# Attention pieces in another order: the value product one unit behind the transposes, the next scores behind it, weight conversions placed one by one

## The chip, the core and the metric

The kernel runs on one core of a Trainium2 chip. The engines named below are PE (TensorE, matrix products), DVE (VectorE), ACT (ScalarE), POOL (GpSimd) and SP (which issues most transfers). Each engine works through its own list of instructions in the order in which the list is written, and waits on semaphores for the others. The metric is the device time of one execution in microseconds (us), lower is better.

## The reference

Three stages: attention with a window of 32 tokens and 32 global tokens per batch, a dense layer with a gated activation, and a routed layer of eight experts.

```python
# attention, B=4, H=8, 512 local and 32 global tokens, head size 64
s_g = scale * q_g @ k_all^T;  out_g = softmax(s_g) @ v_all      # global rows see every key
s_l = concat(scale * q_l @ k_g^T, where(|i-j| <= 32, scale * q_l @ k_l^T, -1e9))
out_l = softmax(s_l) @ concat(v_g, v_l)
x = concat(out_g, out_l)                    # 2304 tokens x 512
# dense layer, 512 -> 2048 -> 512
h = x @ w_in
sp = where(h > 20, h, log1p(exp(min(h, 20))))
y = (h * tanh(sp)) @ w_out
# routed layer: each token goes to one expert, 288 tokens to each
logits = y @ w_gate                         # assigned greedily over the sorted logits
out[mask_e] = relu(y[mask_e] @ w1[e]) @ w2[e]
```

## The kernel before

**Phase 1** does the attention and, between its parts, the first half of the dense layer's 2048 columns. The attention is cut into 24 **pieces**: 16 local ones (128 queries each, `piece`) and 8 global ones (one batch and four heads, `piece_g`). A piece is a Python generator that stops at lettered stages: `q` scores on PE (tile psS), `t` mask and row minimum on DVE (P, mx), `e`/`f` eight exponentials on ACT, `n` row sums inverted on DVE (sm), `a`/`A` transposes of heads 0 to 3 on PE (psA) and their copy on ACT (PAA), `b`/`B` the same for heads 4 to 7 (PAB), `v` value product on PE (psO), `x` scaling on DVE (O), `z` transposes of O on PE (psX) and the split into a high part (ACT, x0h) and a low part (DVE, x0l). In a global piece the tiles are Pg, PgA, PgB and Og. psA has one buffer, so the second transposes wait for the first copy; psO and psX share one buffer.

The dense layer is cut into **chunks**: 256 tokens times 256 hidden columns. A chunk is four **units** of PE work: two of the first product (`m1a`, tiles psH<-x..,wi..; 12 matmuls each) and two of the second (`m1b`, psY<-wo..; 6 matmuls each). Between them stands a chain over ACT and DVE: exponential (me), two DVE steps (mu), Ln and exponential on ACT, two DVE steps (mu, mw), the split into gh (ACT) and gl (DVE). The second product of a chunk comes after the first product of the next one. `gate` steps (psrT, psl) work out routing logits of finished rows.

The dense weights come as 64-bit words and are turned into floats by `load_wide`: a transfer into a staging buffer (wide, three buffers), three DVE steps (wz, L228 to L230), then a high part on ACT (L203) and a low part on POOL (L206). Phase 1 needs 16 such loads: two each of w_in and w_out for four pairs of columns (wi00, wo00 to wi03, wo03).

**What sets the order.** In phase 1 every PE instruction is linked behind the one before it, as the code emits it. For the first three pieces ACT and DVE are linked in the same way; after that a scheduler places their instructions by what they depend on. The order of emission is a string: SEQ0 for each of the first three pieces, SEQ for the rest. `0` is the new piece, `1` the one before it; `w` are two dummy matmuls, `u` one unit, `U` units as long as some are due (5.2 for a local, 3.0 for a global piece), `g` a gate step, and `s` starts one more weight load and advances all that are under way by a step. SP issues transfers in order and waits in that order: `load_qk(t + 2)` stands behind the scores of piece t and waits for them, `load_v(t + 2)` behind the value product of piece t.

**After phase 1** come phase 2 (the rest of the dense layer), the routing and the experts.

Of the kernel before, what the change touches and what calls it, by code (L numbers as in the profile page):

```python
# [15 lines left out]
OP = mybir.AluOpType  # L16
# [3 lines left out]
B, H, SL, SG, D = 4, 8, 512, 32, 64  # L20
# [20 lines left out]
PE, ACT, DVE = mybir.EngineType.PE, mybir.EngineType.Activation, mybir.EngineType.DVE  # L41
LINK = [PE]
WARM = 10
GLOBALS = (4, 5, 8, 10, 11, 12, 13, 14)
CH0 = 3
RATE = {"l": 5.2, "g": 3.0}
LAG = 1
XTRA = 3
WK = 2
CHAIN = 5  # L50
SEQ0 = "0q w 1A 0t w 1B 1v s 0e w 1x 0f 1z s 0n"
SEQ = "u 1A 0n u s 1B 1v u s g u 1x g u s 1z g U"
STAGES = "qtefnaAbBvxyz"
NS = 3
SIDE = "oo ooo - o oo - - i ii i ii - ii"
LOAD_AT = 1
STEP_FILL = 8
# [93 lines left out]
class Build:  # L151
# [158 lines left out]
    def step(s, *new, mid=None):  # L310
# [10 lines left out]
        s.gate((0,))  # L321
        s.turn_all(s.side)

    def link(s, x):
        if s.order is not None and x.ins.engine in s.linked:
            if x.ins.engine in s.order:
                s.tc.add_manual_dep(x.ins, s.order[x.ins.engine],
                                    mybir.DependencyInfo(mybir.DependencyClass.NoSync, mybir.DependencyReason.DATA),
                                    reason="pipeline")
            s.order[x.ins.engine] = x.ins.name  # L330
        return x

# [22 lines left out]
    def piece(s, t):  # L355
        nc = s.nc
        c = t % 4
        qk = s.Q[t]
        mask = s.mask[:, 0 if c == 0 else (2 if c == 3 else 1)]
        pool = s.psE[t % len(s.psE)]  # L360
        psS = [pool.tile([128, 4, 128], F32, name="psS") for _ in range(2)]
        for hp in range(4):
            for u, f in enumerate(FIRST):
                r = slice(u * 32, u * 32 + 32)
                for j in range(2):
                    q = qk[j * 64:(j + 1) * 64, hp]
                    s.link(nc.tensor.matmul(psS[j][r, hp], q[:, r], q[:, 128 + f * 32:256 + f * 32], start=True, stop=True))  # L367
        s.load_qk(t + 2)
        yield "q"
        P = s.ap.tile([128, 8, 128], F32, name="P", bufs=2)  # L370
        mx = s.sp.tile([128, 8], F32, name="mx")
        sm = s.sp.tile([128, 8], F32, name="sm")
        for h in range(8):
            s.link(nc.vector.tensor_tensor_reduce(out=P[:, h], in0=psS[h % 2][:, h // 2], in1=mask, scale=-SCALE, scalar=3e38,  # L374
                                                  op0=OP.add, op1=OP.min, accum_out=mx[:, h:h + 1]))
        yield "t"
        for h in range(8):
            s.link(nc.scalar.activation(P[:, h], P[:, h], AF.Exp, bias=mx[:, h:h + 1], scale=-1.0,  # L378
                                        accum_out=sm[:, h:h + 1]))
            if h == 3:  # L380
                yield "e"
        yield "f"
        s.link(nc.vector.tensor_scalar(sm, sm, 1e-9, None, op0=OP.add))
        s.link(nc.vector.reciprocal(sm, sm))
        yield "n"
        PT = []
        for z, (y, w) in enumerate(("aA", "bB")):
            ps = s.psT.tile([128, 4, 128], F32, name="psA", tag="t")
            for h in range(4):
                s.link(nc.tensor.transpose(ps[:, h], P[:, 4 * z + h], s.ident))  # L390
            yield y
            PT.append(s.ap.tile([128, 4, 128], F32, name="PA" + "AB"[z], tag="P" + "AB"[z], bufs=1))
            s.link(nc.scalar.activation(PT[z], ps, AF.Copy))  # L393
            yield w
        psO = s.psT.tile([128, 8, D], F32, name="psO", tag="x")
        v = s.V[t]
        for h in range(8):
            for u in range(4):
                r = slice(u * 32, u * 32 + 32)
                s.link(nc.tensor.matmul(psO[r, h], PT[h // 4][:, h % 4, r], v[:, u, h * D:(h + 1) * D], start=True, stop=True))  # L400
        s.load_v(t + 2)
        yield "v"
        O = s.ap.tile([128, 8, D], F32, name="O", bufs=1)
        s.link(nc.vector.tensor_tensor(O, psO, sm[:, :, None].to_broadcast([128, 8, D]), op=OP.mult))  # L404
        yield "x"
        px = s.psT.tile([128, 4, 128], F32, name="psX", tag="x")
        for hp in range(4):
            s.link(nc.tensor.transpose(px[:, hp], O[:, 2 * hp:2 * hp + 2].rearrange("p h d -> p (h d)"), s.ident))  # L408
        bi, col = min(t // 2, 7), t - 2 * min(t // 2, 7)
        if bi < 7 and col == 0:  # L410
            s.X[bi] = s.xslots(bi % 3)
        cs = slice(col * 128, col * 128 + 128)
# [31 lines left out]
    def piece_g(s, i):  # L444
# [143 lines left out]
    def phase1(s, p1):  # L588
        nc, tc = s.nc, s.tc
        s.Q, s.V, s.X, s.x_d, s.ready, s.ys = {}, {}, {}, {}, set(), {}  # L590
        pieces = []
        for t in range(16):
            pieces += [("l", t)] + [("g", i) for i, a in enumerate(GLOBALS) if a == t]
        chunks = [(bi, f) for bi in range(6) for f in range(0, FP, 2)]
        with ExitStack() as at:
# [20 lines left out]
            nc.sync.dma_start(s.ident, s.ins["cst"][:, :128])  # L616
            s.load_qk(1)
            s.load_v(0)
            loads = [z for i in range(4) for ld in (s.load_in, s.load_out) for z in ld(0, i, lambda i=i: s.w1[i])]
            s.X[7] = s.xslots(7, 384)  # L620
            s.order, s.linked = {}, [PE, ACT, DVE]
# [25 lines left out]

            n = 0
            acc = 0.0
            old = []  # L650
            while pieces or old:
                s.turn_all(s.tails)
                if n == XTRA:
                    extra.close()
                    s.psE = [s.psS]
                    s.psY = [p1.enter_context(tc.tile_pool(name="psY", bufs=2, space=PSUM, side="right"))] * 2
                p = pieces.pop(0) if pieces else ("g", None)
                new = None if p[1] is None else s.piece(p[1]) if p[0] == "l" else s.piece_g(p[1])
                acc = min(acc + RATE[p[0]], 8) if n >= CH0 else 0
                old[:0] = [new]  # L660
                if n == NS:
                    s.linked, s.static = LINK, False
                cur = 0
                for op in (SEQ0 if n < NS else SEQ).split():
                    if op == "w":
                        idle(WK)
                    elif op == "s":
                        if loads:
                            s.side.append(loads.pop(0))
                        s.turn_all(s.side)  # L670
                    elif op == "u":
                        if acc >= 1 and unit():
                            acc -= 1
                    elif op == "U":
                        while acc >= 1 and unit():
                            acc -= 1
                    elif op == "g":
                        cur = s.gates[0] if s.gates and cur == 0 else cur
                        k = s.at.get(cur, 0)
                        if cur in s.gates:  # L680
                            s.gate((k,))
                            if k == 0:
                                s.gate((1,))
                        cur = cur or None
                    elif int(op[0]) < len(old) and old[int(op[0])]:
                        g = old[int(op[0])]
                        while STAGES.index(op[1]) > at_stage.get(g, -1):
                            at_stage[g] = STAGES.index(next(g, "z"))
                del old[1:]
                if new is None:  # L690
                    old = []
                if n == 0:
                    s.load_v(1)
                    nc.sync.dma_start(s.wg[:, :4 * E].rearrange("p (k e) -> p k e", e=E), s.ins["wg"].rearrange("(k p) e -> p k e", p=128))
                if n == 3:
                    s.load_gk(0)
                    s.load_gv(0)
                n += 1
            assert not loads
            for c, what, _ in units:  # L700
                r = next(c, 0)
                if what is None:
# [536 lines left out]
```

## Time and profile before

| | |
|---|---|
| median of three runs | 871.46 us (868.78 to 872.36) |
| the profiled execution | 868.8 us, span 867.0 us |
| PE busy | 777.0 us, 90% of the span |
| DVE, ACT, POOL busy | 537.8, 429.5, 168.6 us |
| mean granted clock of PE | 0.950 of full speed |
| end of phase 1 (first matmul on x7 after the last piece) | 316.78 us |

The span runs from the first to the last instruction. A row of the chronological view gives the start, the duration, the engine, the line, the operation and its tiles, and in brackets the idle time before it and what ended that. A row of the view of waits gives the total, how often, and the longest. Granted clock 1.00 is 2.4 GHz, and 0.5 would be 1.2 GHz.

### The profile page before, as it was taken

To read this page: it belongs to the slowest core of one execution; us is meant where nothing else is said; L and a number is where in the kernel's file an instruction comes from. 1 tells how busy PE (TensorE), PEld (TensorE's weight loads), DVE (VectorE), ACT (ScalarE), POOL (GpSimd) and SP (SyncE) were. 2 spreads that over 40 slices of the span, in tenths; PEclk is the share of its full clock that TensorE was granted. 3 is DMA by queue.
4 is the path that set the end of the run, shared out by engine and by line. 5 is a ranking of instruction groups with operands and counts; after the bars stand their busy time and mean duration, and the time that the engine had idled before them with its cause. 6 is when DMAs were issued, how large, how long until landed. Compare 5 with 4: busy or idle time off the path is not lost. (4 is left out here: it accounts for less than half of the span.)

```text
span 867.0 us, 18491 instructions
## 1 busy us (share of the span) xinstructions
PE 777.0 (90%) x7496; PEld 675.3 (78%) x7496; DVE 537.8 (62%) x1323; ACT 429.5 (50%) x955; POOL 168.6 (19%) x138
## 2 busy tenths in 40 slices
PE   5767897889998999989999997899879899999995
PEld 2555776767777778878999976677679899999995
DVE  2687755535555548887878767887646555555420
ACT  3465466536565647455656553212246454554420
POOL 0222100000000012143100137634340211222001
PEclk9787899979999999999999999899999999999998
DMA  9879564626543102243113115332467657666101
GB/s 347 316 275 318 182 220 169 238 71 215 198 173 118 42 26 73 74 146 110 50 50 98 50 40 150 50 37 37 110 196 221 197 172 246 196 215 198 50 1 60
DMA packets 44726, 124.30 MB, mean 143 GB/s; under 512 B 5728, under 2 KB 14432, under 8 KB 42592
## 3 DMA queue, kind: packets, MB, share of 16 engines
q1 hardware_dynamic: 37696, 103.45, 35.6%
q0 software_dynamic: 6944, 19.67, 8.9%
q8 instruction: 59, 0.97, 0.5%
q14 instruction: 27, 0.22, 0.1%
HBM read 103.43 MB, written 19.66 MB: 142 GB/s over the span
## 5 line engine op out<-in xcount | busy, mean ns | idle before, releaser
L519 ACT ACTIVATE me<-psH 128x512 f32<-128x512 f32 (+1 forms) x72 | 41.1, 571 | 82.0 <-PE psH L511 79.1
L521 DVE TENSOR_SCALAR mu<-me 128x512 f32<-128x512 f32 (+1 forms) x72 | 34.5, 479 | 55.7 <-ACT me L519 54.6
L378 ACT ACTIVATE P<-P,mx 128x128 f32<-128x128 f32 x128 | 49.5, 388 | 12.8 <-DVE mx L374 12.8
L527 DVE TENSOR_TENSOR mu<-mu,psH 128x512 f32<-128x512 f32 (+1 forms) x72 | 47.0, 653 | 12.3 <-ACT me L524 11.6
L524 ACT ACTIVATE me<-mu,two 128x512 f32<-128x512 f32 (+1 forms) x72 | 49.9, 694 | 8.1 <-DVE mu L522 7.6
L522 DVE SCALAR_TENSOR_TENSOR mu<-me,mu 128x512 f32<-128x512 f32 (+1 forms) x72 | 47.6, 662 | 2.2
L1193 DVE SCALAR_TENSOR_TENSOR hl<-ps2H,hh 128x272 fp32r<-128x272 f32 x64 | 27.2, 437 | 28.6 <-ACT hh L1192 28.4
L1192 ACT ACTIVATE hh<-ps2H 128x272 fp32r<-128x272 f32 x64 | 24.7, 394 | 40.3 <-PE ps2H L1190 40.3
L206 POOL TENSOR_TENSOR wo10l<-wz,wo10h 128x512 fp32r<-128x512 f32 x2 | 2.5, 1289 | 216.7 <-ACT wo10h L203 216.7
L525 ACT ACTIVATE me<-me 128x512 f32<-128x512 f32 (+1 forms) x72 | 43.7, 607 | 1.6
L374 DVE CUSTOM_DVE_ANT_0 P<-psS,mask 128x128 f32<-128x128 f32 x128 | 28.7, 284 | 13.8 <-PE psS L367 13.7
L1171 POOL DMA_INDIRECT out<-ro,idx x17 | 21.9, 1289 | 60.0 <-ACT ro L1170 46.3
L1207 ACT ACTIVATE oT<-ps2O 128x256 f32<-128x256 f32 x32 | 12.1, 378 | 43.1 <-PE ps2O L1205 43.1
L537 DVE TENSOR_TENSOR gl<-mw,gh 128x512 fp32r<-128x512 f32 (+1 forms) x36 | 27.0, 751 | 6.7 <-ACT gh L535 6.1
L1208 DVE COPY orest<-ps2O 128x16 f32<-128x16 f32 x32 | 5.5, 172 | 38.9 <-ACT oT L1207 38.9
L529 DVE TENSOR_TENSOR g<-mu,me 128x512 f32<-128x512 f32 (+1 forms) x36 | 27.2, 755 | 3.9 <-ACT me L525 0.3
L535 ACT ACTIVATE gh<-mw 128x512 fp32r<-128x512 f32 (+1 forms) x36 | 21.7, 603 | 11.6 <-DVE mw L534 11.2
L408 PE MATMUL psX<-ident,O 128*128 128x128 f32 x64 | 11.9, 317 | 16.7 <-DVE O L404 16.7
L400 PE MATMUL psO<-v,PAB 128*32 128x64 f32 x512 | 11.3, 233 | 17.1 <-ACT PAB L393 16.6
L534 DVE TENSOR_TENSOR mw<-mu,me 128x512 f32<-128x512 f32 (+1 forms) x36 | 25.0, 693 | 2.1 <-ACT me L525 0.8
L228 DVE TENSOR_SCALAR wz<-wide 128x512 int32<-128x512 int32 x32 | 16.7, 522 | 14.4 <-DMA wide<-w_in 10.3
L229 DVE SCALAR_TENSOR_TENSOR wz<-wide,wz 128x512 int32<-128x512 int32 x32 | 24.8, 774 | 0.3
(933 smaller groups left out, 2964.3 us busy)
## 6 DMA issues: line engine op xcount, KB each, us to landing
stage<-w SPq DMA_DIRECT2D x64, 512.0 KB, 4.0
v<-v SPq DMA_DIRECT2D x16, 1024.0 KB, 5.3
qk<-qk SPq DMA_DIRECT2D x16, 960.0 KB, 5.4
wide<-w_in SPq DMA_DIRECT2D x16, 512.0 KB, 3.7
wide<-w_out SPq DMA_DIRECT2D x16, 512.0 KB, 4.0
kgl<-kt SPq DMA_DIRECT2D x8, 544.0 KB, 4.1
vgl<-vt SPq DMA_DIRECT2D x8, 512.0 KB, 5.7
y_d<-y1o SPq DMA_DIRECT2D x16, 256.0 KB, 2.8
```

Source lines behind the costliest of these rows:

```text
L374: s.link(nc.vector.tensor_tensor_reduce(out=P[:, h], in0=psS[h % 2][:, h // 2], in1=mask, scale=-SCALE, scalar=3e38, op0=OP.add, op1=OP.mi ...
L378: s.link(nc.scalar.activation(P[:, h], P[:, h], AF.Exp, bias=mx[:, h:h + 1], scale=-1.0, accum_out=sm[:, h:h + 1]))
L519: s.link(nc.scalar.activation(e, ps, AF.Exp))
L521: s.link(nc.vector.tensor_scalar(u, e, E20, 2.0, op0=OP.min, op1=OP.add))
L522: s.link(nc.vector.scalar_tensor_tensor(u, e, E20, u, op0=OP.min, op1=OP.mult))
L524: s.link(nc.scalar.activation(e, u, AF.Ln, bias=s.two))
L525: s.link(nc.scalar.activation(e, e, AF.Exp, scale=-1.0))
L527: s.link(nc.vector.tensor_tensor(u, u, ps, op=OP.mult))
L529: s.link(nc.vector.tensor_tensor(w, u, e, op=OP.mult))
L534: s.link(nc.vector.tensor_tensor(w, u, e, op=OP.mult))
L537: s.link(nc.vector.tensor_tensor(gl, w, gh.bitcast(F32), op=OP.subtract))
L1193: nc.vector.scalar_tensor_tensor(hl[:, f], ps, 0.0, hh[:, f].bitcast(F32), op0=OP.max, op1=OP.subtract)
```

## The change

The parts of the pieces are emitted in another order. In the steady order (SEQ) a unit now stands between the first transposes and the second (`1A g u 1B`), another between the second transposes and the value product (`1B g c c u g 1v`), the scores of the next piece come behind the value product (`1v 1x 0q`) and no longer between the two transposes, and two units stand between these scores and the transposes of O. The addition and reciprocal of the row sums move from stage `n` to behind the value product. Each of the first three pieces has a string of its own. The loads of weights are started, converted and split by three letters of their own (`i`, `c`, `k`), two at a time, instead of by `s`. The global pieces come earlier (behind local pieces 3, 4, 6, 8, ... instead of 4, 5, 8, 10, ...), and two loads (the second v, the first global piece's) are issued earlier.

```diff
-GLOBALS = (4, 5, 8, 10, 11, 12, 13, 14)
+GLOBALS = (3, 4, 6, 8, 10, 11, 12, 13)
...
-SEQ0 = "0q w 1A 0t w 1B 1v s 0e w 1x 0f 1z s 0n"
-SEQ = "u 1A 0n u s 1B 1v u s g u 1x g u s 1z g U"
+SEQ0 = ["i i 0q w 0t w 0f w", "0q w 0t 1A w 1B w 1v 0f 1x c k 1z c k i i",
+        "1A w 1B w 1v 1x 0q 0t c k 1z 0f c k i i u u"]
+SEQ = "1A g u 1B g c c u g 1v 1x 0q k k 0n i i u u c c 1z k k i i U"
...
+    def behind(s, x, name):
+        s.tc.add_manual_dep(x.ins, name if isinstance(name, str) else name.ins.name,
+                            mybir.DependencyInfo(mybir.DependencyClass.NoSync, mybir.DependencyReason.DATA),
+                            reason="pipeline")
...
         yield "f"
-        s.link(nc.vector.tensor_scalar(sm, sm, 1e-9, None, op0=OP.add))
-        s.link(nc.vector.reciprocal(sm, sm))
         yield "n"
...
+                last = s.link(nc.tensor.matmul(psO[r, h], PT[h // 4][:, h % 4, r], v[:, u, h * D:(h + 1) * D], start=True, stop=True))
         s.load_v(t + 2)
         yield "v"
+        s.behind(s.link(nc.vector.tensor_scalar(sm, sm, 1e-9, None, op0=OP.add)), last)
+        s.link(nc.vector.reciprocal(sm, sm))
...
-                    elif op == "s":
+                    elif op == "i":
                         if loads:
-                            s.side.append(loads.pop(0))
-                        s.turn_all(s.side)
+                            wide.append((loads.pop(0), 0))
+                            next(wide[-1][0])
+                    elif op in "ck":
+                        for k, (g, at) in enumerate(wide):
+                            if at == "ck".index(op):
+                                wide[k] = g, at + 1
+                                next(g, 0)
+                                break
```

**PE, a local piece between two local pieces.** First before, in the middle of phase 1; psS are the scores of the next piece, psA the two transposes of the current one, PAA and PAB the two halves of its value product, psX its last transposes:

```order
L390 MATMUL psA<-ident,P 128x128 x4
L367 MATMUL psS<-qk 32x128 x32
L545 MATMUL psY<-wo03h,gh 128x512
...
L390 MATMUL psA<-ident,P 128x128 x4
L400 MATMUL psO<-v,PAA 32x64 x16
L400 MATMUL psO<-v,PAB 32x64 x16
L545 MATMUL psY<-wo03h,gh 128x512
...
L511 MATMUL psH<-x2h,wi01l 128x256
L408 MATMUL psX<-ident,O 128x128 x4
```

The same stretch of the program now, for another local piece (line numbers of the changed kernel):

```order
L391 MATMUL psA<-ident,P 128x128 x4
L284 MATMUL psl<-rT,wg 32x128 x4
L514 MATMUL psH<-x1h,wi02h 128x256
...
L288 MATMUL psl<-ident,gT 128x128
L401 MATMUL psO<-v,PAA 32x64 x16
L401 MATMUL psO<-v,PAB 32x64 x16
L370 MATMUL psS<-qk 32x128 x32
L514 MATMUL psH<-x1h,wi02h 128x256
...
L548 MATMUL psY<-wo01h,gl 128x512
L411 MATMUL psX<-ident,O 128x128 x4
```

A unit has moved in between the second transposes and the value product, the scores have moved behind the value product, and two units follow them before psX.

**ACT, the copies PAA and PAB.** Before, at a local piece in the middle of phase 1 (P,sm are exponentials of the next piece, me, gh are the dense chain):

```order
L393 ACTIVATE PAA<-psA 128x512
L524 ACTIVATE me<-mu,two 128x512
L525 ACTIVATE me<-me 128x512
L378 ACTIVATE P,sm<-P,mx 128x128
L535 ACTIVATE gh<-mw 128x512
L378 ACTIVATE P,sm<-P,mx 128x128 x7
L393 ACTIVATE PAB<-psA 128x512
```

Now, at a local piece (rT, gT belong to the gate steps):

```order
L394 ACTIVATE PAA<-psA 128x512
L527 ACTIVATE me<-mu,two 128x512
L279 ACTIVATE rT<-psrT 128x512
L528 ACTIVATE me<-me 128x512
L394 ACTIVATE PAB<-psA 128x512
L286 ACTIVATE gT<-psl 128x128
L538 ACTIVATE gh<-mw 128x512
L381 ACTIVATE P,sm<-P,mx 128x128 x8
```

The eight exponentials of the next piece stood ahead of PAB and now stand behind it.

**SP, the loads around the third pair of w_in.** Now (v and qk are loads of local pieces, kgl and vgl of a global one, wide are weight loads, x_d stores of finished rows); the first row shown is the load of the fifth v:

```order
L350 DMA v<-v 128x2048
L345 DMA qk<-qk 128x1920
L223 DMA wide<-w_out 128x1024 x2
L223 DMA wide<-w_in 128x4x256
L350 DMA v<-v 128x2048
L223 DMA wide<-w_in 128x4x256
L431 DMA qg<-qg 128x64
L433 DMA kgl<-kt 128x1088
L223 DMA wide<-w_out 128x1024 x2
L223 DMA wide<-w_in 128x4x256
L420 DMA x_d<-x1h 128x1024
L223 DMA wide<-w_in 128x4x256
```

The second half of wi02 has the load of the sixth v ahead of it (before it was the fifth), and the second half of wi03 has a store of x1 ahead of it.

## Rows read from the trace of the kernel before

**Rows 1.** Busy time, granted clock, DMA share, GB/s of each engine in five stretches.
```profile
0.00:40.00 40.00, 24.17 (x392) 14.76 (x393) 17.43 (x76) 16.41 (x59) 5.28 (x8) 0.83 0.91 336
40.00:97.00 57.00, 41.93 (x599) 35.06 (x599) 44.20 (x119) 31.85 (x90) 14.62 (x11) 0.79 0.80 281
97.00:200.00 103.00, 88.34 (x1200) 72.84 (x1199) 53.76 (x173) 55.94 (x160) 1.29 (x1) 0.92 0.48 168
200.00:316.00 116.00, 108.59 (x1564) 87.15 (x1562) 66.79 (x206) 72.13 (x202) 0.00 (x0) 0.99 0.39 135
316.00:336.00 20.00, 19.02 (x120) 16.68 (x123) 11.34 (x25) 12.62 (x27) 3.54 (x3) 1.00 0.14 44
```

**Rows 2.** What PE waited for from 5 to 316 us: total, times, longest.
```profile
PE psX L408 <- DVE O L404: 16.7, 4, 8.5
PE psO L400 <- ACT PAB L393: 16.6, 9, 3.9
PE psO L488 <- ACT PgB L480: 7.5, 7, 1.5
```

**Rows 3.** ACT in order of time, 140 to 152 us.
```profile
143.87 0.40 ACT L378 ACTIVATE P<-P,mx 128x128 f32<-128x128 f32 x1 [0.30 <-DVE mx L374]
...
147.31 0.39 ACT L378 ACTIVATE P<-P,mx 128x128 f32<-128x128 f32 x1
...
147.70 0.57 ACT L393 ACTIVATE PAB<-psA 128x512 f32<-128x512 f32 x1
```

**Rows 4.** PE in order of time, three rows from three places of phase 1.
```profile
23.65 1.11 PE L408 MATMUL psX<-ident,O 128*128 128x128 f32 x4 [8.49 <-DVE O L404]
...
97.10 0.28 PE L511 MATMUL psH<-x1h,wi00h 128*128 128x256 f32 x1
...
148.32 0.65 PE L400 MATMUL psO<-v,PAB 128*32 128x64 f32 x32 [3.92 <-ACT PAB L393]
```

**Rows 5.** DVE in order of time, the first weight conversion and the first O.
```profile
17.36 0.43 DVE L228 TENSOR_SCALAR wz<-wide 128x512 int32<-128x512 int32 x1 [8.52 <-DMA wide<-w_in]
...
22.91 0.68 DVE L404 TENSOR_TENSOR O<-psO,sm 128x512 f32<-128x512 f32 x1
```

**Rows 6.** PE in order of time, 203 to 213 us, a stretch without waits.
```profile
203.50 0.39 PE L511 MATMUL psH<-x0h,wi01h 128*128 128x256 f32 x1
...
204.98 0.60 PE L390 MATMUL psA<-ident,P 128*128 128x128 f32 x4
205.51 0.65 PE L400 MATMUL psO<-v,PAA 128*32 128x64 f32 x32
206.09 0.66 PE L276 MATMUL psrT<-ident,y1o 128*128 128x128 f32 x4
...
209.87 0.48 PE L545 MATMUL psY<-wo00h,gh 128*128 128x512 f32 x1
...
211.34 0.60 PE L471 MATMUL psA<-ident,Pg 128*128 128x128 f32 x4
211.86 1.16 PE L367 MATMUL psS<-qk 64*32 64x128 f32 x64
212.95 0.38 PE L511 MATMUL psH<-x0h,wi02h 128*128 128x256 f32 x1
```

**Rows 7.** Groups of instructions, 0 to 97 us: count, busy us, mean ns, idle before.
```profile
L374 DVE CUSTOM_DVE_ANT_0 P<-psS,mask 128x128 f32<-128x128 f32 x48 | 10.7, 282 | 5.9 <-PE psS L367 5.8
L203 ACT ACTIVATE wi01h<-wz 128x512 fp32r<-128x512 f32 x2 | 1.3, 632 | 5.6 <-DVE wz L230 5.6
L206 POOL TENSOR_TENSOR wi01l<-wz,wi01h 128x512 fp32r<-128x512 f32 x2 | 2.8, 1406 | 4.6 <-ACT wi01h L203 4.6
```

**Rows 8.** Issues of weight loads, 0 to 97 us: count, size, median us to landing.
```profile
wide<-w_in SPq DMA_DIRECT2D x8, 512.0 KB, 8.9
```

**Rows 9.** All weight loads up to 110 us: time to landing.
```profile
DMA to landing us min/median/max: 3.9/5.7/12.5
```

**Rows 10.** The third conversion step up to 110 us: ns, least, median, most.
```profile
L230 DVE SCALAR_TENSOR_TENSOR wz<-wide,wz x18: 675/691/1662, 18.5 to 105.9; 128x512 int32<-128x512 int32 x18
```

More of the change, by code (lines that the diff above doesn't have):

```diff
@@ L50 @@
 CHAIN = 5
-SEQ0 = "0q w 1A 0t w 1B 1v s 0e w 1x 0f 1z s 0n"
-SEQ = "u 1A 0n u s 1B 1v u s g u 1x g u s 1z g U"
+SEQ0 = ["i i 0q w 0t w 0f w", "0q w 0t 1A w 1B w 1v 0f 1x c k 1z c k i i",
+        "1A w 1B w 1v 1x 0q 0t c k 1z 0f c k i i u u"]
+SEQ = "1A g u 1B g c c u g 1v 1x 0q k k 0n i i u u c c 1z k k i i U"
 STAGES = "qtefnaAbBvxyz"
-NS = 3
 SIDE = "oo ooo - o oo - - i ii i ii - ii"
@@ L326, in link @@
             if x.ins.engine in s.order:
-                s.tc.add_manual_dep(x.ins, s.order[x.ins.engine],
-                                    mybir.DependencyInfo(mybir.DependencyClass.NoSync, mybir.DependencyReason.DATA),
-                                    reason="pipeline")
+                s.behind(x, s.order[x.ins.engine])
             s.order[x.ins.engine] = x.ins.name
@@ L399, in piece @@
                 r = slice(u * 32, u * 32 + 32)
-                s.link(nc.tensor.matmul(psO[r, h], PT[h // 4][:, h % 4, r], v[:, u, h * D:(h + 1) * D], start=True, stop=True))
+                last = s.link(nc.tensor.matmul(psO[r, h], PT[h // 4][:, h % 4, r], v[:, u, h * D:(h + 1) * D], start=True, stop=True))
         s.load_v(t + 2)
         yield "v"
+        s.behind(s.link(nc.vector.tensor_scalar(sm, sm, 1e-9, None, op0=OP.add)), last)
+        s.link(nc.vector.reciprocal(sm, sm))
         O = s.ap.tile([128, 8, D], F32, name="O", bufs=1)
@@ L618, in phase1 @@
             s.load_v(0)
+            s.load_v(1)
             loads = [z for i in range(4) for ld in (s.load_in, s.load_out) for z in ld(0, i, lambda i=i: s.w1[i])]
@@ L649, in phase1 @@
             acc = 0.0
+            wide = []
             old = []
@@ L660, in phase1 @@
                 old[:0] = [new]
-                if n == NS:
+                if n == len(SEQ0):
                     s.linked, s.static = LINK, False
                 cur = 0
-                for op in (SEQ0 if n < NS else SEQ).split():
+                for op in (SEQ0[n] if n < len(SEQ0) else SEQ).split():
                     if op == "w":
                         idle(WK)
-                    elif op == "s":
+                    elif op == "i":
                         if loads:
-                            s.side.append(loads.pop(0))
-                        s.turn_all(s.side)
+                            wide.append((loads.pop(0), 0))
[6 more added lines that the diff above has]
+                                break
                     elif op == "u":
@@ L691, in phase1 @@
                     old = []
-                if n == 0:
-                    s.load_v(1)
+                if n == 1:
                     nc.sync.dma_start(s.wg[:, :4 * E].rearrange("p (k e) -> p k e", e=E), s.ins["wg"].rearrange("(k p) e -> p k e", p=128))
-                if n == 3:
+                if n == 2:
                     s.load_gk(0)
@@ L698, in phase1 @@
                 n += 1
-            assert not loads
+            assert not loads and all(at == 2 for _, at in wide)
             for c, what, _ in units:
```

## Prediction

> **What bounds the kernel now.** I read the stretches first. From 316 us on PE is busy 19.02 of 20 us at full clock, and its order of instructions there is the same in both kernels, so what follows phase 1 should just move with its end; 868.8 - 316 = 553 us are taken as fixed. Phase 1 is where PE stands still: 30.9 us in the first 97 (97 less 24.17 and 41.93) and 22.1 us from 97 to 316 [rows 1]. Its clock falls there too: granted 0.83 and 0.79 in the first two stretches, 0.92 in the third, that is, the 1.2 GHz level for part of them, after waits [rows 1].
>
> Then the waits of PE. Three kinds hold 40.8 us: psX for O 16.7, the value product for PAB 16.6, and for PgB 7.5 [rows 2]. The mechanism of the second is seen on ACT around 148 us: eight exponentials of the next piece from 143.87 to 147.70 and only then the copy PAB, while PE stood 3.92 us in front of the value product that reads it [rows 3, 4]. The longest wait, 8.49 us before psX at 23.65, has its cause on DVE: a weight conversion at 17.36 that waited 8.52 us for its transfer held up everything queued behind it, row sums, masks and O [rows 4, 5].
>
> I split phase 1 at 97.1 us, where the first product on x1 begins [rows 4], because up to there weights are being loaded: DMA share 0.91 and 0.80, against 0.48 and 0.39 after it [rows 1].
>
> **What PE has to do after 97 us.** 219 us less 22.1 idle is 196.9 busy. The lower clock stretches that by about 88.34 x 0.08 + 108.59 x 0.01 = 8.2, so about 188.8 us is work at full clock [rows 1].
>
> **The change, later stretch (PE and ACT).** A half chunk of the first product takes 1.48 us (203.50 to 204.98) and of the second 1.47 (209.87 to 211.34), the transposes of four heads 0.53, half a value product 0.58, the scores 1.09 [rows 6].
> - The second transposes are now followed by a unit and the first half of the value product before PAB is read: 1.5 + 0.6 = 2.1 us for a copy of 0.57 [rows 3, 6], with the exponentials now behind the copy. The PAB and PgB waits (24.1 us over phase 1) should go. If ACT's dense chain stands ahead of the copy the cover is thinner, and another short wait remains.
> - psX now has the scores and one or two units between it and the value product, 2.6 to 4 us, for O, 0.68 us on DVE [rows 5], and the two small steps on the row sums, about 1 us in all. That wait should go as well. The moved row sums only fill this gap.
> - What loses cover is the softmax: scores to transposes was about four units and is now two or three plus psX, about 3.4 to 5 us. Needed are two or three masks (10.7/48 = 0.22 us each [rows 7]) and four exponentials of 0.39 [rows 3], some 2.3 us if ACT is free. It holds if no more than two dense steps of 0.6 us stand ahead.
>
> The new waits are unknown. Bounds by the nearest rows: 0.1 us a piece if everything is covered, and 1.1 for each of the 20 pieces left if each stalls as the global ones did at PgB (7.5/7 [rows 2]). I take 0.3, as covers are two to three times what they hide: 6 us, range 2 to 22, the lower clock included.
>
> **The change, earlier stretch.** Here I follow the new orders step by step, with a conversion at 1.9 us on DVE (0.43 [rows 5], two steps of 0.69 [rows 10], and the gaps), 0.63 for the high part on ACT, 1.3 to 1.4 for the low part on POOL [rows 7].
> - First two pieces. O of piece 0 no longer stands behind the conversion, so psX comes at about 16 instead of 23.65. But the conversion still cannot begin before about 17.4 (its transfer, [rows 5]), and the copy PAA of piece 1 now stands on ACT behind both halves of wi00 and x0h: 17.4 + 1.9 + 0.6 + 0.6 + 0.7 + 1.9 + 0.6 = 23.7 less some overlap, say 23. Its second transposes, value product and the scores of piece 2 follow to 27; O, masks, the next conversion, its high part, x0h and four exponentials take ACT to about 34. The first dense matmul starts near 35. The gain of the start has gone.
> - wi01. Its transfers are issued behind two stores that wait for x0l at 33. At the median landing of 8.9 us [rows 8] they are there at 42, converted among the dense chain by 48; POOL ends at 49.6. That chunk's first product ends near 51.
> - wi02. Its second half is issued behind the sixth v, which waits for the value product of piece 3 (near 57), and needs a staging buffer that the conversion of wo01 frees. This stands on DVE behind O of piece 3: about 61.7. At the least landing, 3.9 us [rows 9], it arrives at 65.6; conversion, ACT and POOL end at 69.8, the product at 71.3.
> - wi03. Its second half stands behind the store of x1, whose input is copied at 72.6; two transfers to 78, conversion behind others to 82, ACT and POOL to 84. The product ends near 86.
>
> At that point PE still owes what before had been done by 97.1: one local piece's transposes, value product, psX and next scores (1.06 + 1.16 + 0.5 + 1.09) and one second product of 2.94, 6.7 us [rows 6]. So the early stretch is worth only 97.1 - 86 - 6.7 = 4.4 us: the wait for O turns into waits for weights. Bounds for the 86: 79 if transfers land at their least and DVE is never behind, 95 if each of the three late weights costs 3 us more (landing goes up to 12.5 [rows 9]).
>
> **The sum.** 86 + 6.7 + 188.8 + 6 = 287.5 for the end of phase 1, against 316: 28.5 us less. 868.8 - 28.5 = 840.3, **840 us**. The profiled execution is 2.7 us below the median shown (871.46) and equals the lowest run; the prediction for a median is thus 840 to 843, and I keep 840.
>
> **A rule that speaks against it.** DVE's third conversion step takes 675 ns at least but 1662 at most [rows 10]; POOL's low part beside it took 1406 on average for wi01 [rows 7]. The Trainium skill, page "SBUF — State Buffer", section "Who interferes with whom", says that a DVE instruction with two SBUF inputs and a POOL instruction that reads SBUF exclude each other: the second waits until the first has ended. By that rule conversions placed by twos, right behind the splits of others, meet POOL more often. The trace agrees in its extremes (1662 against 675 ns), not in its median (691). By the rule in every case the sum would be 852, by the median 840; it is the second rival below.
>
> **The rivals.**
> - *The start gains too*: weights land early, and the end of the fourth first product comes at 74 to 79. For it: 3.9 us is possible [rows 9]. Against: SP issues behind waits on PE. 840.3 - 10 = 830, down to 826. Chance 0.13.
> - *Conversions block one another*: one of the two-input steps of each of the 12 weight halves from wi01 to wo03 meets a subtraction and takes 1.0 us more (1662 - 675): 12 us on DVE in the stretch that waits for weights, first stretch 98 instead of 86. 852. For it: the extremes in rows 10; against: the median is 691. Chance 0.16.
> - *Slower*: the DVE list is now the bound. In it O and the masks stand behind the last step of the dense chain (gl), which waits for ACT (gh), which waits for DVE (mw). If each of 20 pieces makes PE wait 3.9 us, as PAB did at worst [rows 2], phase 1 ends at 281.5 + 78 = 359 and the time is 912. It decides from (28.5 + 6)/20 = 1.7 us a piece. Against: DVE is busy 66.8 of 116 us and ACT 72.1 in the later stretch [rows 1], and one chunk's chain has about four units to run in. Chance 0.06.
> - *No change*: what phase 1 gives back is waited for later, since weights or the copies of x come no earlier. 868. Against: DMA is at 0.14 of its share right after phase 1 [rows 1]. Chance 0.05.
>
> **How the numbers follow.** The forecast has the remaining 0.60, with a range of its own from 832 (2 us of waits and an early stretch 4 better) to 850 (16 us of waits). The range for 8 in 10 takes in the first two rivals, 826 to 857. About 0.5%, 4.4 us, is what a measurement of this kernel can tell from no change. Faster: 0.60 + 0.13 + 0.16 = 0.89, less 0.01 for the tail of the second rival, 0.88; same 0.06; slower 0.06.
>
> **What would show it.** Right: no PAB or PgB wait over 1 us after 100 us, psX waits for O gone, granted clock above 0.95 from 100 us on, the last psX near 287. In the early stretch waits on L203 or L206 (weights) instead of O, the end of the product on wi03 near 86. Wrong: transposes that wait for the exponentials (L381), scores that wait for DVE, or a first product on x1 later than 95.

## The result, and the profile after

The changed kernel takes **846.33 us** (median of four runs, 845.11 to 852.61) against 871.12 of the kernel before on the same chip (868.78 to 872.36): ratio 0.9733, 95% interval 0.9681 to 0.9785. The forecast was 840 with a range of 826 to 857. The profiled execution is the one of 845.11 us, with a span of 843.1 and a mean granted clock of 0.957.

Windows of the changed kernel, columns as in [rows 1], cut where its phase 1 ends (the first matmul on x7 behind the last piece starts at 294.32, before at 316.78):

```profile
0.00:40.00 40.00, 25.26 (x396) 16.50 (x397) 16.23 (x72) 17.35 (x61) 5.27 (x8) 0.84 0.90 331
40.00:97.00 57.00, 38.48 (x468) 32.55 (x468) 42.45 (x100) 27.62 (x72) 13.49 (x10) 0.76 0.67 239
97.00:200.00 103.00, 96.74 (x1548) 80.05 (x1548) 66.01 (x216) 67.02 (x198) 2.60 (x2) 1.00 0.63 224
200.00:293.50 93.50, 89.13 (x1338) 73.69 (x1336) 55.32 (x184) 61.30 (x181) 0.00 (x0) 0.98 0.38 133
```

The first 97 us are not better: PE stands still for 33.3 us of them, before for 30.9 [rows 1]. From 97 to the end of phase 1 it stands still for 10.6, before for 22.1, and the clock that had been 0.92 in the third stretch is 1.00.

The waits of PE in the changed kernel, 5 to 300 us (total, times, longest), beside [rows 2]:

```profile
PE psH L514 <- ACT wi02h L203: 8.8, 1, 8.8
PE psA L474 <- ACT Pg L466: 7.5, 5, 2.2
PE psA L391 <- ACT PAA L394: 7.1, 4, 5.8
PE psA L391 <- ACT P L381: 4.6, 1, 4.6
PE psH L514 <- ACT wi03h L203: 3.5, 1, 3.5
PE psH L514 <- ACT wi01h L203: 2.7, 1, 2.7
...
PE psX L411 <- DVE O L407: 1.1, 2, 0.8
```

None for PAB or PgB is left, and 1.1 us for O instead of 16.7. (One more wait of psX, 1.3 us at 102.45, stands under mg, the DVE instruction right behind O; counted with it, it is 2.4.) In their place stand weights (wi01 to wi03), two early waits (5.8 for PAA, 4.6 for exponentials), and, all after 97 us, the waits of the global transposes for Pg.

ACT around 150 us in the changed kernel, to be read beside [rows 3]:

```profile
150.74 0.58 ACT L522 ACTIVATE me<-psH 128x512 f32<-128x512 f32 x1
151.22 0.59 ACT L394 ACTIVATE PAB<-psA 128x512 f32<-128x512 f32 x1
151.70 0.28 ACT L286 ACTIVATE gT<-psl 128x128 f32<-128x128 f32 x1
...
156.92 0.40 ACT L381 ACTIVATE P<-P,mx 128x128 f32<-128x128 f32 x1 [1.30 <-DVE mx L377]
```

The copy comes 5.7 us ahead of the first exponential of the next piece; before it came behind the eighth.

### The profile page after: what moved, and what is told of

The parts are those of the page before. It is cut to its first block, busy times and chain, and to the rows that moved or that the text cites. A ratio compares the mean times of both kernels' runs of the same rounds, so it can differ in the third digit from the quotient of the medians.

```text
span 843.1 us, 18500 instructions
## 1 busy us (share of the span) xinstructions
PE 763.7 (91%) x7494; PEld 669.2 (79%) x7494; DVE 535.4 (64%) x1323; ACT 426.5 (51%) x955; POOL 169.5 (20%) x138
## 5 line engine op out<-in xcount | busy, mean ns | idle before, releaser
L381 ACT ACTIVATE P<-P,mx 128x128 f32<-128x128 f32 x128 | 49.6, 389 | 28.3 <-DVE mx L377 28.3
L391 PE MATMUL psA<-ident,P 128*128 128x128 f32 x128 | 21.4, 290 | 11.8 <-ACT PAA L394 7.1
L391 PEld LDWEIGHTS psA<-ident,P 128*128 128x128 f32 x128 | 15.9, 146 | 16.5 <-ACT PAA L394 9.0
L229 DVE SCALAR_TENSOR_TENSOR wz<-wide,wz 128x512 int32<-128x512 int32 x32 | 26.0, 814 | 0.3
L230 DVE SCALAR_TENSOR_TENSOR wz<-wide,wz 128x512 int32<-128x512 int32 x32 | 25.5, 796 | 0.4
```

## The experiments

The letters of the order strings are those of the section on the kernel before. The experiments were timed beside the kernel before on three chips, where its medians were 870.7 to 871.6 us. "x7" is the start of the first matmul on x7 in the profiled run, the end of phase 1.

| kernel | median us (range) | ratio, 95% interval | x7 |
|---|---|---|---|
| before | 871.12 (868.78 to 872.36) | | 316.78 |
| the change | 846.33 (845.11 to 852.61) | 0.9681 to 0.9785 | 294.32 |
| e1_parts | 853.46 (849.96 to 856.13) | 0.9729 to 0.9834 | 300.62 |
| e2_start | 879.32 (875.07 to 883.00) | 1.0063 to 1.0136 | 324.60 |
| e3_unit | 840.58 (836.47 to 844.14) | 0.9584 to 0.9706 | 283.33 |
| e10_late | 840.84 (838.05 to 849.51) | 0.9600 to 0.9742 | 289.32 |
| e9_unit2 | 849.82 (848.62 to 853.48) | 0.9702 to 0.9783 | 296.53 |
| e4_globals | 860.20 (858.50 to 861.57) | 0.9819 to 0.9900 | 302.67 |
| e13_unit_globals | 847.54 (843.53 to 850.97) | 0.9694 to 0.9766 | 294.88 |
| e5_sums | 844.68 (839.73 to 846.90) | 0.9617 to 0.9723 | 290.15 |
| e6_turns | 843.59 (840.68 to 847.27) | 0.9618 to 0.9723 | 293.52 |
| e7_global | 845.07 (841.59 to 851.10) | 0.9679 to 0.9761 | 290.65 |
| e8_both | 843.20 (840.83 to 845.21) | 0.9642 to 0.9704 | 290.95 |
| e11_three | 863.91 (856.21 to 869.14) | 0.9875 to 0.9941 | 308.57 |

### The order of the parts, and the rest of the change

**e1_parts**: the kernel before with only the new steady order.

```diff
-SEQ = "u 1A 0n u s 1B 1v u s g u 1x g u s 1z g U"
+SEQ = "1A g u 1B g s u g 1v 1x 0q 0n s u u 1z s U"
```

> The kernel before with the steady order of the parts alone (a unit between the two transposes, one between the second transposes and the value product, the next scores behind it); first three pieces, weight loads, row sums and global pieces stay as before. Theory (the gain comes from the later stretch, where the copies PAB and PgB no longer stand behind the exponentials): waits for PAB and PgB after 100 us below 3 us in all, time 848 to 855. Rival (the gain comes from the first three pieces and the letters for the weights): 866 to 873.

Measured 853.46, as the theory had it: 17.7 of the change's 24.8 us come with the steady order alone. From 97 us on no wait for PAB or PgB is left, and one for Pg has come:

```profile
PE psA L471 <- ACT Pg L463: 10.7, 6, 1.9
```

**e2_start**: the changed kernel with the steady order of before; start, load letters and global places stay new.

```diff
-SEQ = "1A g u 1B g c c u g 1v 1x 0q k k 0n i i u u c c 1z k k i i U"
+SEQ = "u 1A 0q k k 0n i i u c c 1B 1v u k k i i g u 1x g u c c 1z g U"
```

> The changed kernel with the steady order of the parts as before (scores between the two transposes, value product right behind the second); its own first three pieces, letters for the weights, row sums and global pieces stay. Theory: the waits for PAB and PgB are back, 15 to 25 us of them, time 862 to 872. Rival (start and weights are the gain): 846 to 852.

Measured 879.32, slower than before by 1.0%: that the waits come back was expected, a time above the kernel before was not. Its waits from 97 us on:

```profile
PE psO L491 <- ACT PgB L483: 15.5, 7, 3.9
PE psO L401 <- ACT PAB L394: 9.3, 8, 3.1
```

The two waits that the change removes are back at once, 24.8 us of them. So the gain is in the steady order; without it everything else in the change costs 8 us.

### Which move of the steady order does it

**e3_unit**: the kernel before, with one unit moved from ahead of the second transposes to behind them. The scores stay where they were, ahead of the second transposes.

```diff
-SEQ = "u 1A 0n u s 1B 1v u s g u 1x g u s 1z g U"
+SEQ = "u 1A 0n s 1B u 1v u s g u 1x g u s 1z g U"
```

> The kernel before with one unit moved from ahead of the second transposes to behind them; the scores stay between the transposes. It parts the unit from the place of the scores. Theory (exponentials of the next piece, 3.1 to 3.8 us, stand ahead of the copy on ACT, so a unit of 1.5 us covers less than half): waits for PAB stay at 5 us or more, time 860 to 868. Rival (the unit between is enough): PAB waits below 2 us, 848 to 856.

Measured 840.58. Theory and rival both fell: one moved unit does more than the whole change. From the first product on x1 to x7 it needs 189.4 us instead of 219.7. PE stands still for 5.14 of them instead of 22.75, and is busy for 184.3 instead of 196.9 with the same matmuls, at a granted clock of 1.00 instead of 0.95 (rows in the next section). Its waits from 97 to 283 us:

```profile
PE psO L400 <- ACT PAB L393: 2.0, 2, 1.5
PE psA L390 <- ACT PAA L393: 0.9, 2, 0.7
```

and ACT at one local piece:

```profile
136.59 0.64 ACT L525 ACTIVATE me<-me 128x512 f32<-128x512 f32 x1
137.13 0.58 ACT L393 ACTIVATE PAB<-psA 128x512 f32<-128x512 f32 x1
137.61 0.39 ACT L378 ACTIVATE P<-P,mx 128x128 f32<-128x128 f32 x1
```

The copy stands ahead of the exponentials here too, although the scores are still emitted ahead of the transposes. With no unit between the scores and the second transposes, these end at 136.0 us, while the first mask of the new piece starts on DVE at 137.20; the copy is ready first in the trace, and it was placed first. (What the scheduler weighs when it places them is not on record, so this reason is argued, not shown.) In the traces of ACT from 97 us on, exponentials of the next piece stand between the two copies at 17 of 18 pieces in the kernel before, at 2 in e3_unit, and at none in e10_late (below) and the change. Both waits of e3_unit are at those two places: 1.5 us at 127.06 with all eight between, 0.5 at 170.55 with two.

**e10_late**: the kernel before with the scores behind the value product and no unit between second transposes and value product.

```diff
-SEQ = "u 1A 0n u s 1B 1v u s g u 1x g u s 1z g U"
+SEQ = "u 1A u 1B 1v 0n s u s g u 1x g u s 1z g U"
```

> The kernel before with the scores of the next piece moved behind the value product and no unit between the second transposes and the value product: the other half of the steady order. On ACT the copies PAA and PAB then stand ahead of the exponentials. Theory (whatever puts the copy ahead of the exponentials removes the long waits; the scores' late place then costs waits of the transposes for the exponentials and for Pg): PAB and PgB waits below 1 us each time, some 0.3 to 0.6 a piece, Pg waits of 8 to 13 us, time 852 to 860. Rival (the late scores do nothing without the unit): 864 or more.

Measured 840.84, again better than expected; no wait for Pg comes after 97 us. Its PAB waits come at ten places from 97 us on, but cost little:

```profile
PE psO L400 <- ACT PAB L393: 3.5, 10, 1.1
```

Late scores put the copy ahead of the exponentials, and what is left is the copy itself, about 0.35 us a place. Either move alone is thus enough, and each gives about 30 us. What they share is the copy's place on ACT.

**e9_unit2**: e2_start with the same one unit moved.

```diff
-SEQ = "u 1A 0q k k 0n i i u c c 1B 1v u k k i i g u 1x g u c c 1z g U"
+SEQ = "u 1A 0q k k 0n i i c c 1B u 1v u k k i i g u 1x g u c c 1z g U"
```

> The changed kernel with the scores back between the transposes and one unit between the second transposes and the value product; it differs from the run with the old steady order (879) by the place of one unit. Theory (the scores' late place is what costs 7.5 us of Pg waits after 97 us, the unit is what gains): Pg waits gone, PAB and PgB waits below 4 us after 100 us, time 838 to 846. Rival (the early scores are only good with the start and the global pieces of before): 852 or more.

Measured 849.82: the unit is worth 29.5 us here (from 879.32) and 30.5 in the kernel before (from 871.12 to 840.58). The time is slower than the theory gave: around the same order, the change's other parts together cost 9 us (849.82 against 840.58). The waits for Pg are gone, as expected, but 5.5 us for PAB are left, at three places (1.7, 2.8 and 0.9), the only three after 97 us where the eight exponentials stand between the copies again. A unit ahead of the value product does not cover them there.

### The global pieces

**e4_globals**: the changed kernel with the old places of the global pieces.

```diff
-GLOBALS = (3, 4, 6, 8, 10, 11, 12, 13)
+GLOBALS = (4, 5, 8, 10, 11, 12, 13, 14)
```

> The changed kernel with the global pieces where they were before (4, 5, 8, 10 to 14). Theory (their place only shifts the same waits): within 4 us of the changed kernel, 842 to 850. Rival (the early global pieces are part of the gain, as they fill the time of the weights): 851 or more.

Measured 860.20, the rival's side: the earlier places are worth 13.9 us in the changed kernel, which the prediction had not priced at all. Only half of it is seen where the edit acts: phase 1 ends 8.4 us later, and what follows it takes 8.3 longer (859.8 less 302.67, against 843.1 less 294.32), for a reason that stays open (last section). In phase 1, from 97 us on:

```profile
PE psA L474 <- ACT Pg L466: 9.9, 6, 2.2
PE psrT L276 <- ACT y1o L583: 3.0, 2, 1.9
```

**e13_unit_globals**: e3_unit with the new places.

```diff
-GLOBALS = (4, 5, 8, 10, 11, 12, 13, 14)
+GLOBALS = (3, 4, 6, 8, 10, 11, 12, 13)
```

> The kernel before with one unit moved behind the second transposes (840.58 by itself), and with the global pieces as early as in the changed kernel. In the changed kernel the earlier global pieces were worth 14 us (860.2 without them). Theory (they pay only where the global pieces' transposes wait for Pg; here PE is busy for 99.61 of 103 us and 82.94 of 85 after 97, and no such wait is left, so at most 5 us are to be had): 838 to 844. Rival (the earlier places are worth as much in any order, since they spread units over the pieces): 826 to 833.

Measured 847.54, worse than e3_unit by 7.0 us: outside what either expected, the same edit with the other sign. From 97 us on it waits where e3_unit did not:

```profile
PE psO L400 <- ACT PAB L393: 5.5, 3, 2.8
PE psY L545 <- ACT gh L535: 2.9, 1, 2.9
```

The PAB waits are again at the three pieces after 97 us that have the eight exponentials between the copies. Phase 1 ends 11.6 us later than in e3_unit (294.88 against 283.33), while in the changed kernel the same places brought its end forward by 8.4. The place of a global piece has no price of its own: it depends on the order around it. Set beside e9_unit2 (849.82, the same global places and the same place for the unit, new start and letters), the new start costs 2.3 us, which the intervals do not tell from nothing; set beside e1_parts (853.46, old places in both), e4_globals puts it at 6.7. In phase 1 alone it is 1.7 and 2.1 us. It gains in neither.

**e7_global**: where the next piece is a global one, one unit more stands between its scores and its transposes, taken from between the two transposes.

```diff
+SEQG = "1A g 1B g c c u g 1v 1x 0q k k 0n i i u u c c 1z k k i i U"
...
-                for op in (SEQ0[n] if n < len(SEQ0) else SEQ).split():
+                for op in (SEQ0[n] if n < len(SEQ0) else SEQG if p[0] == "g" and p[1] is not None else SEQ).split():
```

> The changed kernel, but where the next piece is a global one, no unit stands between the first and the second transposes, and that unit comes behind the psX transposes, ahead of the global piece's own first transposes. Theory (the waits of the first transposes for Pg, 14.9 us at three places of the changed kernel and 7.5 of them at one, come from too few units between the scores of a global piece and its transposes): one unit more (1.5 us) in this gap brings these waits under half, to 7 us or less, phase 1 ends 4 to 8 us earlier, time 838 to 842. Rival (ACT is behind because of its whole load, so that a wait taken away here comes back at the second transposes for PAA or at the value product): the waits only change their names, time 844 to 849.

(This expectation misreads the row of waits: 7.5 us is the total of the changed kernel, at five places; there are no 14.9.) Measured 845.07, not to be told from 846.33. From 97 to 293 us:

```profile
PE psA L392 <- ACT PAA L395: 5.5, 7, 2.1
PE psA L475 <- ACT Pg L467: 1.2, 1, 1.2
```

The cause of the Pg waits was rightly named, since one unit brings them from 7.5 to 1.2. But the second transposes, which lost that unit, now wait for PAA: 5.5 instead of 1.1. The rival holds, most of the gain changed its name.

**e11_three**: no unit between the second transposes and the value product, and none between the two transposes either (the expectation names only the first of these); one more unit behind the scores, and the other ahead of the next transposes, in all pieces.

```diff
-SEQ = "1A g u 1B g c c u g 1v 1x 0q k k 0n i i u u c c 1z k k i i U"
+SEQ = "1A g 1B g c c g 1v 1x 0q k k 0n i i u u u c c 1z k k i i U"
```

> The changed kernel with the unit between the second transposes and the value product moved behind the next scores, in all pieces. What then covers PAB is half a value product of 0.6 us and a gate step, with the exponentials still behind the copy. Theory (the place of the copy ahead of the exponentials is what removed the PAB waits, and units are worth more behind the scores): waits for Pg under 7 us, PAB waits of about 1 us at up to ten pieces, time 838 to 844. Rival (the unit between the transposes and the value product is needed, as the prediction had it): PAB waits of 1 to 2 us at most pieces, 20 to 30 us, time 850 to 862.

Measured 863.91, at the upper end of the rival's range or just above it, but not for its reason:

```profile
PE psB L480 <- ACT PgA L477: 8.3, 7, 1.9
PE psA L391 <- ACT PAA L394: 7.5, 11, 1.3
...
PE psA L474 <- ACT Pg L466: 0.3, 1, 0.3
```

Pg is nearly gone (0.3), PAB is no matter (0.2 us: half a value product stands ahead of its reader), and the first copies PAA and PgA, for which the second transposes wait and which now have no unit to hide behind, cost 15.8. A copy whose reader would come right behind needs a unit in between, and there are about five units for a piece: what one gets another lacks.

### The rest

**e5_sums**: the row sums back at stage `n`.

```diff
+        s.link(nc.vector.tensor_scalar(sm, sm, 1e-9, None, op0=OP.add))
+        s.link(nc.vector.reciprocal(sm, sm))
         yield "n"
...
-        s.behind(s.link(nc.vector.tensor_scalar(sm, sm, 1e-9, None, op0=OP.add)), last)
-        s.link(nc.vector.reciprocal(sm, sm))
```

> The changed kernel with the addition and reciprocal of the row sums back at their stage ahead of the value product. Theory (two small DVE steps in a covered place): 844 to 849, no difference. Rival (they delay what stands behind them on DVE): 850 or more.

Measured 844.68: the move of the row sums is worth nothing that can be told.

**e6_turns**: the weight loads in another order, w_in of the third pair ahead of w_out of the second, and so on; units fall due by the new order.

```diff
-            loads = [z for i in range(4) for ld in (s.load_in, s.load_out) for z in ld(0, i, lambda i=i: s.w1[i])]
+            loads = {(k, i): list(ld(0, i, lambda i=i: s.w1[i])) for i in range(4) for k, ld in enumerate((s.load_in, s.load_out))}
+            turns = [(0, 0), (1, 0), (0, 1), (0, 2), (1, 1), (0, 3), (1, 2), (1, 3)]
+            loads = [z for t in turns for z in loads[t]]
...
```

> The changed kernel with the weight loads in another turn: w_in of the third pair ahead of w_out of the second, w_in of the fourth ahead of w_out of the third. Theory (the wait of 8.8 us before the first product with wi02 is one for the transfer and conversion of its second half, which stand behind the sixth v and behind wo01 on DVE): that wait falls below 3 us, the product on x1 starts 5 to 9 us earlier, time 837 to 842. Rival (the wait moves to wo01 or wi03): 844 to 848.

Measured 843.59, between the two. The wait for wi02 fell from 8.8 to 4.9 us, and new ones for wo02 came (2.1 and 1.6). The first product on x1 starts at 94.83 instead of 95.81: the wait moves from one weight to the next.

**e8_both**: e6_turns and e7_global together.

> The kernel before this one (global pieces with one unit more behind their scores) together with the other order of the weight loads (w_in of the third pair ahead of w_out of the second). The second alone gave 843.59 against 846.33 of the changed kernel. Theory (one edit acts before 97 us, the other after it, so they add): 835 to 840. Rival (what is gained early is waited for again, as the DVE and ACT lists are the same ones): no better than the better of the two alone, 840 to 844.

Measured 843.20: no better than the better of the two alone. The two simplest kernels, e3_unit and e10_late, have the lowest medians of all. The runs of e3_unit (836.47 to 844.14) lie wholly below those of the change (845.11 to 852.61).

## Why the prediction was right, and where not

**PAB, PgB and O.** Right: 24.1 and 16.7 us became 0 and 1.1. The reason given had two halves: "a unit + half a value product" as cover, "with the exponentials now behind the copy". The second half is what the runs show. With the copy ahead of the exponentials e10_late has no unit there and waits 3.5 us in all; where the eight exponentials stand between the copies, e3_unit, e9_unit2 and e13_unit_globals have the unit and still wait, 0.9 to 2.8 us a time. The prediction took the scores' late place and the units ahead of the value product both for needed; either brings the copy forward. Together they leave too few units between a global piece's scores and its transposes: e1_parts and the change, which have both, wait for Pg (10.7 and 7.5 us after 97), e9_unit2 and e10_late, which have one of the two, do not, and one unit put back there (e7_global) leaves 1.2.

**The clock.** Right: 1.00 and 0.98 after 97 us, against 0.92 and 0.99 [rows 1]. By the mean granted clock the low level cost 8.2 us in this stretch before and 1.8 now (89.13 x 0.02), beside waits that fell by 11.5 (22.1 to 10.6).

**New waits: mis-sized, hidden by another term.** Taken as 6 us. The rows show 10.6 us of standing still and 1.8 of lower clock, 12.4 in all. The softmax loses cover, as was said, but at the global pieces, which the sum of masks and exponentials did not look at: transposes for Pg, 7.5 us. On the other side PE's work was less than the 188.8 + 6.7 = 195.5 put down: from 92.28, where the product on wi03 ends, to 293.5 it is busy 190.59 us, 188.8 at full clock. The two misses nearly cancel: 201.2 us from there to the end, 201.5 forecast, which is luck. The 6.7 us owed were there, as 2914 matmuls against 2761 show; the 188.8 was too high. Columns as above, from the first product on x1 (in the changed kernel from the end of wi03) to the end of phase 1, in the kernel before, the changed one, e3_unit and e10_late:

```profile
97.10:316.77 219.67, 196.92 (x2761) 159.93 (x2759) 120.47 (x380) 128.62 (x363) 1.29 (x1) 0.95 0.43 150
92.28:293.50 201.22, 190.59 (x2914) 157.84 (x2912) 125.23 (x408) 131.80 (x385) 2.60 (x2) 0.99 0.50 177
93.90:283.30 189.40, 184.26 (x2762) 151.60 (x2760) 118.61 (x379) 127.38 (x364) 1.29 (x1) 1.00 0.49 174
99.10:289.30 190.20, 184.66 (x2761) 152.47 (x2760) 118.17 (x375) 127.31 (x364) 0.00 (x0) 1.00 0.49 172
```

At a granted clock of 1.00 the same matmuls take 184.3 and 184.7 us. So the stretch before held some 12.7 us more than its work, where the mean clock gave 8.2, and the term of 188.8 was about 4.5 too high. The other 2 us of the difference stay open.

**The early stretch: the step that failed by size.** The forecast had the first dense matmul near 35 (35.33), the product on wi01 ending at 51 (52.2), on wi02 at 71.3 (75.29), on wi03 at 86 (92.28). These 6.3 us carry the end of phase 1 to 293.5 instead of 287.5, and the time to 845 in the profiled execution instead of 840. By the prediction's own account (6.7 us owed at that point) the early stretch then lost 1.9 us instead of gaining 4.4. The pairs e4_globals and e1_parts, e9_unit2 and e13_unit_globals agree that the new start does not pay.

Where wi02 and then wi03 fell behind is seen on SP, DVE and POOL. First SP:

```profile
57.68 0.33 SPq L350 DMA_DIRECT2D v<-v  x1
61.55 0.38 SPq L223 DMA_DIRECT2D wide<-w_in  x1
...
77.24 0.38 SPq L223 DMA_DIRECT2D wide<-w_in  x1
```

then DVE:

```profile
65.18 1.63 DVE L230 SCALAR_TENSOR_TENSOR wz<-wide,wz 128x512 int32<-128x512 int32 x1
67.77 0.21 DVE L469 TENSOR_SCALAR smg<-smg 128x1 f32<-128x1 f32 x1 [0.96 <-ACT Pg L467]
67.90 1.20 DVE L228 TENSOR_SCALAR wz<-wide 128x512 int32<-128x512 int32 x1
...
82.47 1.50 DVE L229 SCALAR_TENSOR_TENSOR wz<-wide,wz 128x512 int32<-128x512 int32 x1
...
86.45 1.54 DVE L230 SCALAR_TENSOR_TENSOR wz<-wide,wz 128x512 int32<-128x512 int32 x1
```

and POOL:

```profile
64.82 1.44 POOL L206 TENSOR_TENSOR wo01l<-wz,wo01h 128x512 fp32r<-128x512 f32 x1 [1.29 <-ACT wo01h L203]
67.55 1.27 POOL L206 TENSOR_TENSOR wi02l<-wz,wi02h 128x512 fp32r<-128x512 f32 x1 [1.29 <-ACT wi02h L203]
71.29 1.45 POOL L206 TENSOR_TENSOR wi02l<-wz,wi02h 128x512 fp32r<-128x512 f32 x1 [2.48 <-ACT wi02h L203]
...
88.74 1.28 POOL L206 TENSOR_TENSOR wi03l<-wz,wi03h 128x512 fp32r<-128x512 f32 x1 [1.29 <-ACT wi03h L203]
```

The transfer of wi02's second half went out at 61.55, as forecast (61.7), behind the sixth v, and took 3.8 us. But DVE came to it only at 67.90. Ahead of it stood a conversion step of 1.63 us and the row sum of a global piece, which waited 0.96 us for ACT; the conversion's own first step then took 1.20. POOL ended at 72.74, forecast 69.8. The 1.20 and the 1.63 both lie beside a POOL subtraction (67.55 and 64.82), where the same steps alone take 0.42 and 0.69. The Trainium skill, page "SBUF — State Buffer", section "Who interferes with whom", says that a DVE instruction that uses the port pair shared with GpSimd and a GpSimd instruction exclude each other; the trace agrees at these places. It agrees elsewhere too: of the 54 conversion steps up to 110 us nine are longer than their median by over 0.15 us, and each of the nine lies beside a subtraction on POOL. Together the 54 steps take 39.8 us (37.8 in the kernel before), where 18 times 0.42 + 0.69 + 0.69 would be 32.4. So the second rival came in part: 7.4 us on DVE instead of its 12.

The clock, which the early steps of the prediction left out, adds to it. PE on wi02 and wi03, and then three windows with columns as above:

```profile
67.52 0.58 PE L514 MATMUL psH<-x0h,wi02h 128*128 128x256 f32 x1 [8.85 <-ACT wi02h L203]
...
69.68 0.41 PE L514 MATMUL psH<-x0h,wi02l 128*128 128x256 f32 x1
69.89 0.41 PE L514 MATMUL psH<-x0h,wi02h 128*128 128x256 f32 x1
...
85.89 0.58 PE L514 MATMUL psH<-x0h,wi03h 128*128 128x256 f32 x1 [3.52 <-ACT wi03h L203]
...
92.00 0.28 PE L514 MATMUL psH<-x0h,wi03l 128*128 128x256 f32 x1
```

```profile
67.50:78.00 10.50, 9.19 (x35) 8.21 (x36) 7.46 (x13) 3.03 (x7) 2.72 (x2) 0.50 0.37 129
78.00:82.40 4.40, 4.37 (x115) 3.09 (x113) 2.90 (x6) 2.73 (x6) 1.63 (x2) 0.98 0.98 303
85.89:91.70 5.81, 5.00 (x21) 4.70 (x22) 3.37 (x16) 3.79 (x17) 2.81 (x2) 0.50 0.91 362
```

After the wait of 8.85 us the matmuls follow one another every 0.21 us; in [rows 6] twelve take 1.48, 0.123 each. That is the 1.2 GHz level, granted 0.50 up to 78.0. Then the clock is full, and behind the wait of 3.52 us it is at the low level again up to 91.7.

The 6.3 us can now be taken apart. The product on wi02 ends 4.0 us late (75.29 against 71.3): 2.9 because POOL ended late, 1.1 because its last ten matmuls take from 72.79 to 75.09 where ten at 0.123 take 1.2. The second half of wi03, behind the store of x1, lands at 82.40 (77.24 and 5.2 for the transfer) instead of 78, 0.4 more. From there POOL needs 7.6 us, to 90.02, instead of 6: the two steps of 1.50 and 1.54 beside POOL are that 1.6. The last ten matmuls, again at the low level, add 0.3. So DVE steps beside POOL cost at least 2.4 of the 6.3 (0.8 for the step of 1.20, and 1.6), the clock some 1.4, and the other 2.5 are the later landing (0.4) and the DVE list, in which the row sum that waits for ACT stands ahead.

**The signs that were named.** Most of those for right came: no PAB or PgB wait, the clock, waits for weights in the early stretch; the end of wi03 (92.28) and the last psX (292.98) came 6 us late. But two of the three for wrong came as well: transposes that wait for the exponentials (L381, 4.6 us, once, before psA at 34.04; in the later stretch those for Pg), and a first product on x1 later than 95, at 95.81. The account of the early stretch was wrong, and that the time came as near as it did is in part luck: the work was put too high.

**After phase 1.** Taken as fixed at 553 us. In the changed kernel it is 548.8 of the span, before 550.2: good enough here, not in general (below).

**Rivals.** The start that gains, the slower DVE list and no change did not come; the second rival came in part (above). The two edits to the loads and the global covers that the last runs tried (e6 to e8) gained about 3 us at most: what remains early is the chain from transfer over DVE and ACT to POOL.

## What to carry to other kernels

Where one engine copies between two matrix products, look first at what stands ahead of the copy in that engine's list: one unit of other work moved from ahead of the second transposes to behind them gave 30 us, more than a rewritten order with a dozen moves. Units of filler are a budget, so one that covers one copy can uncover another; count for every reader of a copy, the rare pieces too. A part of a change that is worth 14 us in one order can cost 7 in another, so price parts in the order in which they will run.

## What the runs showed of the hardware that was not expected

Waits were paid twice here. After 8.85 us of standing still PE ran at the 1.2 GHz level for 10.5 us more, up to 78.0, though it was busy for 9.19 of them, and after 3.52 us for 5.8 more. Over phase 1 it adds up: from the first product on x1 on, e3_unit stands still for 17.6 us less than the kernel before (5.14 against 22.75), and it is busy for 12.7 us less with the same matmuls.

What follows phase 1, the same instructions in every kernel, took from 548.7 us of the span (e2_start, e10_late) to 557.1 (e4_globals); e3_unit, with 555.5, gave back there 5 us of the 33 that its phase 1 had gained on the kernel before. The wait that differs most is that for gathered rows in the expert stage: 4.0 us in the changed kernel, 5.0 in e3_unit, 7.2 in e9_unit2. It does not make up the whole difference (3.9 us before, so 1.1 of e3_unit's 5). What sets it was not tried, and both stay open.
